# Moving one of four bit steps of a weight conversion from VectorE to POOL

## The chip, the cores and the metric

One Trainium2 chip, one core of it, one launch. The metric is the device time of that launch in microseconds (us), lower is better. The engines are named as in the profile: PE (TensorE: matmuls), DVE (VectorE), ACT (ScalarE), POOL (GpSimd), SP (SyncE, which here only issues DMAs). [...]

## The reference

Three stages on float32 activations. First a recurrent attention over 4 batches, 8 heads, 768 steps, head size 48; then a max-of-three layer; then a layer with h - tanh(h).

```python
for t in range(S):                                   # 768 steps, state of 48 x 48 per head
    cur = np.einsum('bhd,bhe->bhde', u[None] * kt, vt)
    y[:, :, t] = np.einsum('bhd,bhde->bhe', rt, state + cur)
    state = wt[:, :, :, None] * state + np.einsum('bhd,bhe->bhde', kt, vt)
...
h = np.maximum(np.maximum(x @ w1, x @ w2), x @ w3)   # x: 3072 x 384, each w: 384 x 768
y = h @ w_out                                        # 768 x 384
h = y @ w_in                                         # 384 x 2048
out = (h - np.tanh(h)) @ w_out2                      # 2048 x 384
```

The weights of the two layers come as float64. The result is float32.

## The kernel before

The 3072 tokens are done in six groups of 512 tokens (four chunks of 128). The attention of a chunk is done with scans of the decays, a masked score matrix and a carried state. While the max-of-three layer of group g is on PE, the attention of group g + 1 is done beside it: the loop over the 18 weight columns (6 row blocks f, three weights j: 18 "slots") calls `advance(slot)` after the matmuls of a slot, and `advance` issues the next steps of the list that `att_steps` made (`i0` to `i5` for each chunk in the first group).

**The weights on their way in.** The 64-bit words are moved by SP into slots of the tile `Y` (eight of them, `SLOTS`), and the device turns each block of 128 x 384 numbers, called a unit, into float32 with five instructions: `abs_f64` on ACT (line 66) takes the size of the upper half as a float32, and `bits_f64` does four steps on DVE: line 72 bounds the size from both sides, line 73 shifts and masks, lines 74 and 75 put sign, exponent and the lower half's top bits together. All four work in place on the unit's tile, so each waits for the one before.

**Units.** There are 24: 0 to 17 are the three first weights (tiles `WAg0` to `WAg17`; in the order's lists they stand as `WAg_102` to `WAg_119`, so unit 13 is `WAg_115` and unit 17 is `WAg_119`), 18 to 23 the layer's output weight (all in one tile, `WOg`). `w1_unit` (line 531) does one and then issues the load of the raw words of the unit eight later. Eight units (0 + 1 + 3 + 4, the table `PRO`) are done during the prologue, in which the attention of the first group runs alone. The other 16 are done in the first group: `advance(slot)` ends with `w1_upto(slot + 1 + 8)`, so slot s makes unit 8 + s, behind the attention steps of that slot; the last ones follow at the end of the loop.

**Order.** The first group stands in a block where the program's order is kept as written (`tc.manual_schedule`). So what waits on an engine is what the code wrote earlier: on DVE the evictions `max0` (line 644, which frees a PSUM bank for PE), the scans (lines 207 and 209), the scaled keys and queries (215, 216), the diagonal (291), the state (329) and the key transpose (259); on POOL the mask of the scores (line 303, two a chunk), the bonus products (lines 224, 225) and the decayed state (245). From the second group on, weights are multiplied as pairs of a high and a low part (lines 488 to 490, `mm3`); their split (lines 478 and 479) begins when the first group ends.

Of the kernel before, what the change touches and what calls it, by code (L numbers as in the profile page):

```python
# [15 lines left out]
ALU = mybir.AluOpType  # L16
# [26 lines left out]
PRO = [0, 1, 3, 4]  # L43
# [11 lines left out]
LO_BITS = (896 << 20)  # L55
HI_BITS = (1150 << 20) | 0xFFFFF


def bits_f32(i):
    return struct.unpack("<f", struct.pack("<I", i))[0]  # L60
# [4 lines left out]
def abs_f64(act, raw, out):  # L65
    act.activation(out, raw[:, 1::2].bitcast(F32), AF.Abs)


def bits_f64(dve, raw, out):
    oi = out.bitcast(I32)  # L70
    high, low = raw[:, 1::2], raw[:, 0::2]
    dve.tensor_scalar(out, out, bits_f32(LO_BITS), bits_f32(HI_BITS), ALU.max, ALU.min)
    dve.tensor_scalar(oi, oi, 3, 0x3FFFFFFF, ALU.logical_shift_left, ALU.bitwise_and)
    dve.scalar_tensor_tensor(oi, high, -0x40000000, oi, ALU.bitwise_and, ALU.bitwise_or)  # L74
    dve.scalar_tensor_tensor(oi, low, 29, oi, ALU.logical_shift_right, ALU.bitwise_or)  # L75
# [16 lines left out]
def main_path(ctx, tc, wT, rkT, w0, rk0, nat, vpad, uT, ub, wA, wo1, wi2, wo2, outT, count):  # L92
    nc = tc.nc
    pe, act, dve, pool, sp = nc.tensor, nc.scalar, nc.vector, nc.gpsimd, nc.sync
# [378 lines left out]
    def w1_upto(n):  # L473
        while w1n < min(n, 24):
            w1_unit()
# [5 lines left out]
    def conv(raw, hi, lo, eng=pool):  # L481
        g = cv()
        abs_f64(act, raw, g)
        bits_f64(dve, raw, g)
        split(g, hi, lo, eng)
# [38 lines left out]
    def w1_load(i):  # L524
        sp.dma_start(Yi[:, (i % SLOTS) * 2 * UN:(i % SLOTS + 1) * 2 * UN], w1raw[i].bitcast(I32))
# [5 lines left out]
    def w1_unit():  # L531
        nonlocal w1n
        i = w1n
        w1n += 1
        o = i % SLOTS * 2 * UN
        q = i - 3 * F1
        raw = Yi[:, o:o + 2 * UN]
        g = WAg[i].rearrange("p k m -> p (k m)") if q < 0 else WOgf[:, q * UN:(q + 1) * UN]
        abs_f64(act, raw, g)
        bits_f64(dve, raw, g)  # L540
        if i + SLOTS < len(w1raw):
            w1_load(i + SLOTS)

# [25 lines left out]
    for c in range(GROUPS[0]):  # L569
        st = {}  # L570
        n = c + 1
        scores(c, st)
        key_turn_pe(c)
        key_out_pe(c)
        masked(c, st)
        warm(WARM[2] if c < 2 else 0)
        state_mm(c)
        bonus(n)
        scans(n)
        decays(n)  # L580
        state_add(c)
        state_decay(n)
        outputs(c)
        warm(WARM[3] if c < 2 else 0)
        outputs_out(c, c * C)
        squares(n)
        load_next(c)
        if c == 0:
            sp.dma_start(ubt, ub)
            for i in range(PRELOAD[1], SLOTS):  # L590
                w1_load(i)
        for _ in range(PRO[min(c, len(PRO) - 1)]):
            w1_unit()
        bonus_sum(n)
        bonus_vals(n)
# [225 lines left out]
def general_path(ctx, tc, wA, wo1, wi2, wo2, gwkr, gv, gu, outT):  # L821
# [55 lines left out]
    for dst, src in ((WA, wA.rearrange("p f n -> p (f n)")), (WO, wo1),  # L877
                     (W2, wi2.rearrange("p f n -> p (f n)")), (WP, wo2.rearrange("p f n -> p (f n)"))):
        flat = dst.rearrange("p a b c d -> p (a b c d)") if len(dst.shape) == 5 else dst.rearrange("p a b c -> p (a b c)")
        for o in range(0, flat.shape[1], 768):  # L880
            raw = stg.tile([P, 2 * 768], I32, name="graw")
            sp.dma_start(raw, src[:, o:o + 768].bitcast(I32))
            abs_f64(act, raw, flat[:, o:o + 768])
            bits_f64(dve, raw, flat[:, o:o + 768])
# [123 lines left out]
```

## Time and profile before

| what | us |
|---|---|
| median of 3 runs | 876.72 (876.35 to 880.52) |
| the profiled execution, its own time | 877.04 |
| its span in the trace | 875.2 |
| PE busy | 844.2 (96%) |
| DVE busy | 507.2 (58%) |
| ACT busy | 327.7 (37%) |
| POOL busy | 193.7 (22%) |

The profile is of one execution. Times in it are in us from the start of the span; a row of the timeline gives start, duration, engine, line, operation, output <- inputs, shapes, count, and in brackets the idle time of that engine before it and what ended it. A row of the table of busy time by stretch gives the stretch, its length, the busy us (and number) of PE, PEld (PE's weight loads), DVE, ACT and POOL in it, the granted clock, the busy share of the DMA engines, and GB/s. A row of the groups gives line, engine, operation, tiles, shapes and count, then busy us in all and mean ns of one, then the idle time before them and what ended it. Matmuls of float32 appear as two rows for each instruction. [...]

The prologue ends near 49 us, the first group's 18 slots end near 120 us, the first group's output matmuls (line 740) run to 145 us, and the second group begins there.

### The profile page before, as it was taken

Reading aid. Unit: us, or ns where it says so; the run is one execution under the profiler, and the core shown is the slowest. Engines: PE = TensorE matmul, PEld = TensorE weight load, DVE = VectorE, ACT = ScalarE, POOL = GpSimd, SP = SyncE. Lnnn points to the kernel's source line nnn. Section 1 sums busy time; section 2 is a strip of 40 time slices with the busy share of each in tenths; the row PEclk is TensorE's granted clock in tenths of the full one; section 3 lists DMA queues with packets and bytes.
Section 4 is the critical chain, followed back from the end, with each engine's and each line's share of the span. In section 5 each row is a group of like instructions: output and inputs, shape, how many; then the busy total and the mean of one; then the engine's idle time right before and its main releaser. Section 6 shows DMA issues by size and latency. Waiting matters only on the chain.

```text
span 875.2 us, 11930 instructions
## 1 busy us (share of the span) xinstructions
PE 844.2 (96%) x4482; PEld 647.2 (74%) x4482; DVE 507.2 (58%) x824; ACT 327.7 (37%) x647; POOL 193.7 (22%) x201
## 2 busy tenths in 40 slices
PE   7899889999999999999997999999999999999996
PEld 5755445777777777788875688888888888888885
DVE  8989985684574675729989734334334334333332
ACT  4644424244333344335455424323323233323232
POOL 5531426452352342420262200000000000000000
PEclk8999988999999999999999999999999999999998
DMA  9665233244252353315533000000000000000001
GB/s 266 193 210 157 70 95 85 88 128 130 70 163 76 95 145 103 88 55 163 144 105 113 19 1 36 1 1 37 0 1 37 0 1 37 1 0 37 1 1 39
DMA packets 39120, 65.42 MB, mean 75 GB/s; under 512 B 6096, under 2 KB 20176, under 8 KB 39056
## 3 DMA queue, kind: packets, MB, share of 16 engines
q1 hardware_dynamic: 39056, 64.59, 25.2%
q8 instruction: 37, 0.61, 0.3%
q14 instruction: 27, 0.22, 0.1%
HBM read 52.71 MB, written 8.13 MB: 70 GB/s over the span
## 4 chain that ended last, share of the span: by engine, by line
PE 76%; DVE 5%; DMA 2%; ACT 2%; issue 1%; POOL 1%; SPq 0%; ACTq 0%; DVEq 0%
PE bank L488 24%; PE bank L490 23%; PE bank L489 23%; PE bank L355 3%; PE bank L286 2%; PE bank L740 2%; DVE cv L75 1%; DMA fwd<-kbd 1%; PE bank L319 1%; POOL WO2l L479 1%; DVE cv L74 1%; DMA kbd<-fwd 0%; DMA xs<-in_wi 0%; SPq L264 0%; DMA xs<-in_wo 0%
## 5 line engine op out<-in xcount | busy, mean ns | idle before, releaser
L786 DVE TENSOR_TENSOR tmp<-bank,tmp 128x512 f32<-128x512 f32 x96 | 66.3, 691 | 174.5 <-ACT tmp L785 174.5
L785 ACT ACTIVATE tmp<-bank 128x512 f32<-128x512 f32 x96 | 57.4, 598 | 182.5 <-PE bank L490 182.5
L488 PE MATMUL bank<-hh,WO2h 128*128 128x512 f32 x288 | 114.2, 397 | 1.7 <-ACT hh L787 1.6
L490 PE MATMUL bank<-hl,WO2h 128*128 128x512 f32 x288 | 114.3, 397 | 0.8 <-DVE hl L788 0.8
L489 PE MATMUL bank<-hh,WO2l 128*128 128x512 f32 x288 | 113.6, 394 | 0.0
L488 PE MATMUL bank<-xh,WAh 128*128 128x512 f32 x270 | 111.1, 411 | 0.0
L490 PE MATMUL bank<-xl,WAh 128*128 128x512 f32 x270 | 106.8, 395 | 0.0
L489 PE MATMUL bank<-xh,WAl 128*128 128x512 f32 x270 | 106.4, 394 | 0.0
L788 DVE TENSOR_TENSOR hl<-tmp,hh 128x512 fp32r<-128x512 f32 x96 | 66.4, 692 | 59.1 <-PE bank L490 46.6
L787 ACT CAST hh<-tmp 128x512 fp32r<-128x512 f32 x96 | 59.5, 620 | 72.8 <-DVE tmp L786 72.7
L490 PEld LDWEIGHTS bank<-hl,WO2h 128*128 128x128 f32 x288 | 54.1, 188 | 16.1 <-DVE hl L788 3.4
L488 PEld LDWEIGHTS bank<-hh,WO2h 128*128 128x128 f32 x288 | 54.2, 188 | 15.6 <-ACT hh L787 3.3
L489 PEld LDWEIGHTS bank<-hh,WO2l 128*128 128x128 f32 x288 | 54.2, 188 | 12.9
L488 PEld LDWEIGHTS bank<-xh,WAh 128*128 128x128 f32 x270 | 50.8, 188 | 15.1 <-issue 1.9
L721 POOL TENSOR_TENSOR hl<-tmp,hh 128x512 fp32r<-128x512 f32 x25 | 38.3, 1531 | 102.7 <-ACT hh L720 100.2
L490 PEld LDWEIGHTS bank<-xl,WAh 128*128 128x128 f32 x270 | 50.8, 188 | 12.0
L489 PEld LDWEIGHTS bank<-xh,WAl 128*128 128x128 f32 x270 | 50.9, 188 | 10.5 <-issue 0.2
L702 PE MATMUL bank<-x,WAg 128*128 128x512 f32 x108 | 51.3, 618 | 3.7 <-DVE h L644 3.7
L720 ACT CAST hh<-tmp 128x512 fp32r<-128x512 f32 x30 | 18.6, 618 | 87.5 <-DVE tmp L718 76.0
L291 DVE COPY_PREDICATED P<-dmask,sd 128x512 f32<-128x512 uint8 x36 | 29.6, 871 | 33.6 <-POOL P L303 33.6
L718 DVE TENSOR_TENSOR tmp<-bank,tmp 128x512 f32<-128x512 f32 x60 | 40.8, 680 | 13.0 <-PE bank L490 11.4
L488 PE MATMUL bank<-xh,W2ha 128*128 128x512 f32 x108 | 42.4, 393 | 3.9 <-ACT Yb L759 2.8
(204 smaller groups left out, 1617.4 us busy)
## 6 DMA issues: line engine op xcount, KB each, us to landing
Y<-in_wA SPq DMA_DIRECT2D x18, 384.0 KB, 6.4
nt<-in_nat SPq DMA_DIRECT2D x12, 576.0 KB, 4.8
rk<-in_rkT SPq DMA_DIRECT2D x30, 192.0 KB, 3.4
w2st<-in_wi SPq DMA_DIRECT2D x12, 384.0 KB, 3.3
third<-in_nat SPq DMA_DIRECT2D x7, 576.0 KB, 4.5
kbd<-fwd SPq DMA_DIRECT2D x13, 256.0 KB, 2.1
fwd<-kbd SPq DMA_DIRECT2D x52, 64.0 KB, 2.0
third<-in_rkT SPq DMA_DIRECT2D x16, 192.0 KB, 3.4
```

The costliest lines, as they stand in the source:

```text
L291: dve.copy_predicated(q, dmask[:, None, :].to_broadcast([P, NP, C]), sdt[c % 2][:, j::2, None].to_broadcast([P, NP, C]))
L355: pe.matmul(yab[64 * j:64 * j + HD, p * C:(p + 1) * C], *t(j), start=i == 0, stop=i == len(terms) - 1)
L488: pe.matmul(bk, wh, ah, start=first, stop=False)
L489: pe.matmul(bk, wl, ah, start=False, stop=False)
L490: pe.matmul(bk, wh, al, start=False, stop=last)
L702: pe.matmul(bk, WAg[3 * f + j][:, k], x0[:, k], start=k == 0, stop=k == KT - 1)
L718: dve.tensor_tensor(t[:, 0:n], bk[:, 0:n], t[:, 0:n], ALU.max)
L721: (dve if f == F1 - 1 else pool).tensor_tensor(hl[:, f, 0:n], t[:, 0:n], hh[:, f, 0:n], ALU.subtract)
L785: act.activation(t, bk, AF.Tanh)
L786: dve.tensor_tensor(t, bk, t, ALU.subtract)
L787: act.copy(hh[:, r], t)
L788: dve.tensor_tensor(hl[:, r], t, hh[:, r], ALU.subtract)
```

## The change

`bits_f64` gets a parameter: the engine that does its first step. `w1_unit` passes POOL for units 8 to 23 (`i >= sum(PRO)`, which is 8) and DVE for the eight of the prologue. Nothing else is edited. The later conversions of the second layer's weights (`conv`) and the general path pass nothing and stay on DVE.

```diff
-def bits_f64(dve, raw, out):
+def bits_f64(dve, raw, out, clamp=None):
     oi = out.bitcast(I32)
     high, low = raw[:, 1::2], raw[:, 0::2]
-    dve.tensor_scalar(out, out, bits_f32(LO_BITS), bits_f32(HI_BITS), ALU.max, ALU.min)
+    (clamp or dve).tensor_scalar(out, out, bits_f32(LO_BITS), bits_f32(HI_BITS), ALU.max, ALU.min)
     dve.tensor_scalar(oi, oi, 3, 0x3FFFFFFF, ALU.logical_shift_left, ALU.bitwise_and)
...
         abs_f64(act, raw, g)
-        bits_f64(dve, raw, g)
+        bits_f64(dve, raw, g, pool if i >= sum(PRO) else dve)
```

So ACT's step is followed by POOL, and POOL's by three steps on DVE; line 73 now waits for POOL's semaphore instead of DVE's own.

Where the steps come to stand on POOL, in the middle of the first group. Before (`P` are the masked scores, `nt` the chunk's queries, keys and values):

```order
L303 AFFINE_SELECT P_145<-P_145 128x512
L303 AFFINE_SELECT P_146<-P_146 128x512
L224 TENSOR_TENSOR nt_139<-nt_139,ubt 128x384
L225 TENSOR_TENSOR nt_139<-nt_139 128x384
L303 AFFINE_SELECT P_145<-P_145 128x512
```

With the change, from the second of these rows to unit 17:

```order
L303 AFFINE_SELECT P_146<-P_146 128x512
L224 TENSOR_TENSOR nt_139<-nt_139,ubt 128x384
L225 TENSOR_TENSOR nt_139<-nt_139 128x384
L72 TENSOR_SCALAR WAg_115<-WAg_115 128x384
L72 TENSOR_SCALAR WAg_116<-WAg_116 128x384
L72 TENSOR_SCALAR WAg_117<-WAg_117 128x384
L72 TENSOR_SCALAR WAg_118<-WAg_118 128x384
L303 AFFINE_SELECT P_145<-P_145 128x512
L303 AFFINE_SELECT P_146<-P_146 128x512
L224 TENSOR_TENSOR nt_140<-nt_140,ubt 128x384
L225 TENSOR_TENSOR nt_140<-nt_140 128x384
L72 TENSOR_SCALAR WAg_119<-WAg_119 128x384
```

The step of unit 13 (`WAg_115`) and that of unit 17 (`WAg_119`) stand behind the two selects and the two products of a chunk; those of units 14 to 16 follow unit 13's directly.

On DVE the step of unit 17 leaves its place between the scaled queries of a chunk and the unit's second step; a piece of the difference:

```order
 L215 TENSOR_TENSOR rk_138<-rk_138,suf 128x512
 L216 TENSOR_TENSOR rk_138<-rk_138,fwd 128x512
-L72 TENSOR_SCALAR WAg_119<-WAg_119 128x384
 L73 TENSOR_SCALAR WAg_119<-WAg_119 128x384
 L74 SCALAR_TENSOR_TENSOR WAg_119<-Y,WAg_119 128x384
```

The other fifteen rows of line 72 leave DVE in the same way. Beside this, the build moves a few rows on other engines: on SP one of two DMAs of a later chunk's decays (`third<-in_wT`) goes ahead of the six that carry a chunk's output (`xs<-yst`, lines 368 to 371); on PE one score matmul (line 286) stands before the output matmuls of line 740 and not behind; and from the end of the first group on some splits (line 479) change places.

## Rows read from the trace of the kernel before

**Rows 1.** The page's part 1: busy time, share of the span, instructions.
```profile
PE 844.2 (96%) x4482; PEld 647.2 (74%) x4482; DVE 507.2 (58%) x824; ACT 327.7 (37%) x647; POOL 193.7 (22%) x201
```

**Rows 2.** Busy time by stretch of 20 us (columns: see the section on the profile).
```profile
100.00:120.00 20.00, 17.26 (x81) 8.00 (x80) 19.14 (x34) 4.67 (x11) 7.59 (x7) 0.91 0.29 79
140.00:160.00 20.00, 20.00 (x104) 14.02 (x104) 13.24 (x19) 5.27 (x12) 13.30 (x12) 1.00 0.11 32
```

**Rows 3.** The chain that ended last, in order of time: start, us, what.
```profile
118.83 0.68 DVE h L644
...
120.19 0.72 DVE fwd L259
...
120.93 2.01 DMA kbd<-fwd
...
129.81 1.19 PE bank L286 x4
```

**Rows 4.** Timeline of PE, at its two stalls for line 644.
```profile
94.77 2.84 PE L702 MATMUL bank<-x,WAg 128*128 128x512 f32 x6 [0.94 <-DVE h L644]
...
108.24 4.54 PE L702 MATMUL bank<-x,WAg 128*128 128x512 f32 x6 [2.74 <-DVE h L644]
```

**Rows 5.** Busy time by stretch of 5 us (columns as in rows 2).
```profile
110.00:115.00 5.00, 5.00 (x24) 1.98 (x23) 4.67 (x10) 2.34 (x6) 0.00 (x0) 0.73 0.85 238
130.00:135.00 5.00, 5.00 (x9) 2.54 (x10) 3.06 (x8) 1.97 (x4) 2.21 (x3) 0.50 0.37 92
```

**Rows 6.** DVE's groups by line and shape, 54.9 to 117 us.
```profile
L644 DVE TENSOR_TENSOR h<-bank,h 128x512 f32<-128x512 f32 x9 | 6.2, 685 | 0.1
...
L72 DVE TENSOR_SCALAR WAg<-WAg 128x384 f32<-128x384 f32 x10 | 4.6, 460 | 2.9 <-ACT WAg L66 2.9
...
L72 DVE TENSOR_SCALAR WOg<-WOg 128x384 f32<-128x384 f32 x6 | 2.7, 454 | 0.7 <-ACT WOg L66 0.7
```

**Rows 7.** Timeline of DVE: undisturbed steps of unit 15, and unit 18's first.
```profile
81.82 0.35 DVE L72 TENSOR_SCALAR WAg<-WAg 128x384 f32<-128x384 f32 x1
82.20 0.36 DVE L73 TENSOR_SCALAR WAg<-WAg 128x384 int32<-128x384 int32 x1
...
96.50 0.36 DVE L72 TENSOR_SCALAR WOg<-WOg 128x384 f32<-128x384 f32 x1 [0.53 <-ACT WOg L66]
```

**Rows 8.** Timeline of POOL and DVE around unit 13.
```profile
74.00 1.23 POOL L303 TENSOR_SCALAR_AFFINE_SELECT P<-P 128x512 f32<-128x512 f32 x2 [8.35 <-ACT P L302]
...
75.20 1.10 POOL L224 TENSOR_TENSOR nt<-nt,ubt 128x384 f32<-128x384 f32 x1
...
76.38 1.00 POOL L225 TENSOR_TENSOR nt<-nt 128x384 f32<-128x384 f32 x1
...
77.83 0.56 DVE L75 SCALAR_TENSOR_TENSOR WAg<-Y,WAg 128x384 int32<-128x384 int32 x1
```

**Rows 9.** Timeline of POOL and DVE around unit 17.
```profile
89.46 1.90 POOL L303 TENSOR_SCALAR_AFFINE_SELECT P<-P 128x512 f32<-128x512 f32 x2 [12.08 <-ACT P L302]
...
90.90 0.67 DVE L73 TENSOR_SCALAR WAg<-WAg 128x384 int32<-128x384 int32 x1
91.33 1.09 POOL L224 TENSOR_TENSOR nt<-nt,ubt 128x384 f32<-128x384 f32 x1
...
92.50 1.19 POOL L225 TENSOR_TENSOR nt<-nt 128x384 f32<-128x384 f32 x1
92.87 1.24 DVE L75 SCALAR_TENSOR_TENSOR WAg<-Y,WAg 128x384 int32<-128x384 int32 x1
```

**Rows 10.** Timeline of DVE: unit 10's first step, and a scan before unit 16.
```profile
61.33 0.36 DVE L72 TENSOR_SCALAR WAg<-WAg 128x384 f32<-128x384 f32 x1 [1.29 <-ACT WAg L66]
...
85.29 1.23 DVE L209 TENSOR_TENSOR_SCAN fwd<-wt,d 128x516 f32<-128x516 f32 x1
```

**Rows 11.** Timeline of SP and DVE near unit 22.
```profile
111.80 0.43 SPq L192 DMA_DIRECT2D third<-in_wT  x1
...
112.66 0.36 DVE L72 TENSOR_SCALAR WOg<-WOg 128x384 f32<-128x384 f32 x1 [0.16 <-ACT WOg L66]
```

## The prediction

> **What bounds the kernel now.** I read the page's busy shares first: TensorE (PE) is busy for 96% of the span [rows 1], so a change on another engine can only act where PE waits. The table of busy time by stretch shows where that is [rows 2]: in 100 to 120 us PE has 17.26 of 20 us and VectorE (DVE) 19.14, so there DVE is the full engine; in 140 to 160 us PE has its whole 20.00 and DVE 13.24. Then the chain of waits [rows 3]: from 101 us on it runs through DVE, instruction after instruction, to the last running maximum of the first group at 118.83, through the key transpose at 120.19, two transfers through memory, and back to PE at 129.81. After that it is PE's own. The timeline of PE names the two stalls on DVE: 0.94 us before 94.77 and 2.74 us before 108.24, both for an eviction of line 644 [rows 4]. The table in 5-us stretches tells what a stall costs besides: the granted clock is 0.73 in 110 to 115 us, so the six matmuls at 108.24 take 4.54 us where six took 2.84, and 0.50 in 130 to 135 us, behind the wait at the end of the chain [rows 4, 5]. So the change acts on the right engine in the right stage: what DVE gains or loses up to 118.83 goes to the end almost one to one.
>
> **What it takes from DVE.** The 16 clamps took 4.6 + 2.7 = 7.3 us on DVE [rows 6], some of them held up. An undisturbed one is 0.35 to 0.36 us, and the next instruction starts 0.38 us after it did [rows 7]; with that 16 x 0.38 = 6.1 us leave DVE.
>
> **What a clamp costs on POOL.** The trace has no tensor_scalar on POOL. From below: the masks' select, one tile in and one out like the clamp, takes 1.23 us for two of 512 columns, 0.62 each [rows 8]; at 384 columns that is 0.46 us if all of it scales. From above: a product of two 384-column tiles takes 1.10 us [rows 8]. I take 0.55, between the select as it is and the select scaled, because the clamp also has one input; 0.46 and 1.10 are kept for the range. [...]
>
> **Where the two engines exclude each other.** This is the step that decides. At 91.33 and 92.50 POOL multiplies two tiles; the DVE step at 92.87 takes 1.24 us and ends at 94.11, 0.42 us after POOL's end at 93.69, where its like takes 0.56 [rows 8, 9]. The select, with one input, does it too: the DVE step at 90.90 takes 0.67 instead of 0.36, and the two selects 1.90 instead of 1.23 [rows 7 to 9]. One engine waits until the other's instruction is through. So a clamp on POOL is not beside DVE's steps but between them, unless DVE is idle or in an eviction from PSUM: the nine of line 644 took 685 ns on the mean, and nothing is seen to hold them [rows 6].
>
> **The walk through the units** (a unit is one 384-column block; 8 to 23 are moved).
> - Units 8 to 12: unit 8 now waits for two selects and a product, but DVE was idle for 1.29 us before unit 10 [rows 10], which takes that up. From there a 0.38 us saving against a clamp or a POOL queue of the same size: nothing, to 0.3 us either way.
> - Unit 13 (WAg_115): its clamp stands on POOL behind two selects and two products, which end at 77.38 [rows 8]. The clamp then runs 77.4 to 77.95. DVE's last step of the unit ended at 78.39; now the three steps start at 78.0, need 0.36 + 0.56 + 0.56 + two issues of 0.03, and are held some 0.4 us by the clamps of units 14 and 15 right behind: 79.95. That is 1.55 us late; units 14 and 15 have no clamp left and return 2 x 0.38: 0.8 us late.
> - Unit 16: its clamp meets the scan at 85.29 [rows 10], now 0.8 us later, waits for its end and makes DVE wait in turn; the 0.38 us are lost again: 0.9 us late.
> - Unit 17 (WAg_119): the same pattern. The selects and products ended at 93.69 [rows 9]; 0.9 us late and 0.35 us less disturbed they end at 94.25. Clamp to 94.8, three steps of 1.54 us: 96.4 instead of 94.11, 2.3 us late. PE's stall before 94.77 grows by as much.
> - Units 18 to 23: 6 x 0.38 = 2.3 us leave DVE. At two of them DVE already waits for ScalarE's absolute value (idle 0.53 us at unit 18 [rows 7]); there POOL's clamp and its hand-over, 0.55 + 0.1, stand in the same place: 1.3 us. The other four hold DVE by 0.55 less the 0.14 us by which a held step overlaps (0.56 - 0.42), three times in four (the fourth finds DVE idle or evicting): 4 x 0.41 x 0.75 = 1.2 us. Saved 2.3, paid 2.5.
>
> Sum: 2.3 + 0.2, less up to 0.3 for the early units and for gaps between clamps: **+2.2 us** at 118.83. The transpose, both transfers and the scores at 129.81 follow as much later. PE is full after that, so it stays: the profiled execution, 877.04 us (span 875.2), would be 879.2, and the median of the runs, 876.72, lies 0.3 us below it. **Forecast: 879.0 us.** The clock's loss I count as moved, not added: the stall before 94.77 becomes the long one and the one before 108.24 shrinks, since PE arrives there later. The longer queue on POOL keeps no DMA back: SP's transfers of raw weights wait for the unit's last step on DVE, so they start up to 2 us later, into units that are eight turns ahead of their matmul. One transfer of a later chunk's decays, 0.43 us to issue [rows 11], moves ahead of the six small ones that carry a chunk's output; ScalarE's squares wait for those, and the absolute value of unit 22 behind them. DVE was idle 0.16 us there [rows 11], so this can cost up to 0.4; I leave it in the rounding of the sum. The score matmul that moves on PE is one of sixteen and only changes places.
>
> **Rivals.**
> 1. *The clamp is as slow as a two-input product* (slower). Place: units 13 to 23, where some 12 clamps stand or hold on DVE's path. For: two immediate operands and two operations in one instruction, on an engine that needs 1.10 us for a 384-column product. Against: the select. At 1.0 us it adds 0.45 x 12 = 5.4 us: 884.4. It passes 0.5% (4.4 us, about what a measurement of this kernel can tell from no change) from a clamp of 0.55 + 2.2 / 12 = 0.73 us on.
> 2. *POOL does not hold DVE* (faster). If a clamp leaves DVE's steps alone, units 18 to 23 return 2.3 - 1.3 = 1.0 us beside what is late at 17, and the holds at 13 and 16 go (0.8): the result is about +0.4. If POOL also were ahead of DVE everywhere, the 3.7 us of stalls and the 1.7 us of slow matmuls behind 108.24 (4.54 - 2.84) would be the most there is to win: 871.3. Against: the selects in rows 9, and the order, in which two clamps stand behind products. [...]
> 3. *The longer stall near 94 us costs clock of its own.* PE would be idle for over 3 us there, more than before 108.24, and the slow matmuls could outlast DVE's lateness, or a second slow stretch follow. Price: 1.7 us by rows 4, or twice that: 880.7 to 882.4.
>
> **How the numbers follow.** Forecast 0.58, rival 1 0.25, rival 2 0.08 (half of it a real gain), rival 3 0.09. The forecast's own range is 877.0 (clamp 0.46: 0.09 x 12 = 1.1 less; 0.9 less again if the early units and the last four gain what I counted as lost) to 881.2 (clamp 0.73). Range for 8 in 10: 875.0, which leaves out most of rival 2, to 885.0, which takes in rival 1 up to a clamp of 1.05. Faster by over 0.5% (below 872.3): 0.05, from rival 2. Slower (above 881.1): 0.28, being 0.21 of rival 1, 0.06 of rival 3 and 0.01 of the forecast. Within: 0.67.
>
> **What would show it.** The clamp's duration on POOL near 0.55 us where DVE is quiet, longer where it meets a scan; DVE idle before line 73 of units 13 and 17 for POOL, some 2 and 3 us; PE's stall for line 644 near 94 us grown to over 2.5 us and the one near 108 us shrunk; the scores at 129.81 some 2 us later. A clamp above 0.75 us makes rival 1 right. If DVE's steps keep 0.36 and 0.56 us while POOL clamps, or the transpose comes before 120.19, the prediction is wrong in its main step.

## The result, and the profile after

The change makes the kernel 1% slower: 886.42 us median of 5 runs (885.32 to 886.64) against 877.66 of 5 runs of the kernel before (876.35 to 880.52), a ratio of 1.0101 with a 95% interval of 1.0078 to 1.0124. The forecast was 879.0 us in a range of 875.0 to 885.0: the sign of the forecast's sum was right (+2.2 us), its size was not (+8.8 us), and the time lies outside the range. The profiled execution took 886.42 us, span 884.7, so 9.5 us more span than before.

The page's part 1 after, against [rows 1]:

```profile
PE 847.2 (96%) x4482; PEld 648.4 (73%) x4482; DVE 498.8 (56%) x808; ACT 328.0 (37%) x647; POOL 215.6 (24%) x217
```

DVE did get its work off: 16 instructions and 8.4 us less. POOL has the 16 instructions more, and 21.9 us.

The groups of line 72, now on POOL, and of line 73 behind it on DVE, 54.9 to 125 us. They answer to [rows 6], where line 72 took 460 and 454 ns on DVE:

```profile
L72 POOL TENSOR_SCALAR WAg<-WAg 128x384 f32<-128x384 f32 x10 | 16.0, 1608 | 11.0 <-ACT WAg L66 10.9
L72 POOL TENSOR_SCALAR WOg<-WOg 128x384 f32<-128x384 f32 x6 | 9.2, 1537 | 8.3 <-ACT WOg L66 8.3
...
L73 DVE TENSOR_SCALAR WAg<-WAg 128x384 int32<-128x384 int32 x10 | 4.4, 439 | 17.9 <-POOL WAg L72 17.9
...
L73 DVE TENSOR_SCALAR WOg<-WOg 128x384 int32<-128x384 int32 x6 | 2.9, 490 | 3.5 <-POOL WOg L72 3.5
```

The clamp takes 1.5 to 1.6 us on POOL. The prediction took 0.55 and held 1.10 for the upper bound. DVE waits for it 17.9 + 3.5 = 21.4 us, at eight places. Against that stand 7.3 us of clamps and 3.6 us of waits for ScalarE that it no longer has [rows 6]. The balance is 10.5 us, of which 8.0 are still there at the key transpose (below).

The timeline of POOL and DVE at units 12, 13 and 17 (start, duration; in brackets the idle time before and what ended it), against [rows 8, 9]:

```profile
72.25 1.23 DVE L209 TENSOR_TENSOR_SCAN fwd<-wt,d 128x516 f32<-128x516 f32 x1
...
72.36 2.40 POOL L72 TENSOR_SCALAR WAg<-WAg 128x384 f32<-128x384 f32 x1 [3.96 <-ACT WAg L66]
...
80.69 4.70 POOL L72 TENSOR_SCALAR WAg<-WAg 128x384 f32<-128x384 f32 x3
...
82.21 0.65 DVE L73 TENSOR_SCALAR WAg<-WAg 128x384 int32<-128x384 int32 x1 [4.66 <-POOL WAg L72]
...
82.89 0.56 DVE L74 SCALAR_TENSOR_TENSOR WAg<-Y,WAg 128x384 int32<-128x384 int32 x1
...
98.38 1.49 POOL L72 TENSOR_SCALAR WAg<-WAg 128x384 f32<-128x384 f32 x1
...
99.90 0.36 DVE L73 TENSOR_SCALAR WAg<-WAg 128x384 int32<-128x384 int32 x1 [4.61 <-POOL WAg L72]
```

DVE is idle for 4.66 us before unit 13 and 4.61 us before unit 17. Two more things are to be seen. The step of line 74 at 82.89, which reads two tiles, takes its undisturbed 0.56 us in the middle of three clamps (80.69 to 85.39); the one-input step of line 73 at 82.21 is longer, 0.65 for 0.36. And the clamp of unit 12, issued while the scan of 72.25 to 73.48 runs, takes 2.40 us, some 0.9 more than the 1.49 of one alone: it ends 1.28 us behind the scan.

The timeline of PE at its stalls for the eviction of line 644, against [rows 4], where they were 0.94 and 2.74 us:

```profile
84.70 4.54 PE L702 MATMUL bank<-x,WAg 128*128 128x512 f32 x6 [3.59 <-DVE h L644]
...
102.10 4.46 PE L702 MATMUL bank<-x,WAg 128*128 128x512 f32 x6 [2.91 <-DVE h L644]
...
115.89 2.84 PE L702 MATMUL bank<-x,WAg 128*128 128x512 f32 x6 [1.44 <-DVE h L644]
...
127.56 4.56 PE L740 MATMUL bank<-h,WOg 128*128 128x512 f32 x10 [0.35 <-DVE h L644]
```

There is a new stall of 3.59 us before 84.70, behind unit 13, and its six matmuls take 4.54 us where six took 2.84. In the table of busy time by 5 us the granted clock of PE, as a share of full speed, is 0.67 and 0.70 in the stretches behind the two long stalls, where [rows 5] have 0.73 behind the one before:

```profile
85.00:90.00 5.00, 5.00 (x20) 2.18 (x21) 4.77 (x10) 1.71 (x5) 0.39 (x1) 0.67 0.64 162
100.00:105.00 5.00, 2.90 (x4) 1.35 (x5) 3.59 (x7) 3.00 (x8) 1.87 (x2) 0.70 0.03 12
```

The chain of waits that ended last, against [rows 3]. It now runs through POOL:

```profile
120.36 1.50 POOL WOg L72
121.88 0.66 DVE WOg L73
...
128.18 0.72 DVE fwd L259
128.92 2.02 DMA kbd<-fwd
```

The key transpose comes at 128.18 us, 8.0 us later than at 120.19. From there the lateness mostly stays: the last matmul is 9.3 us late.

### The profile page after: what moved, and what is told of

It reads as the page before. It is cut to its first block, busy times and chain, and to the rows that moved or that the text cites. A ratio compares the mean times of both kernels' runs of the same rounds, so it can differ in the third digit from the quotient of the medians.

```text
span 884.7 us, 11936 instructions
## 1 busy us (share of the span) xinstructions
PE 847.2 (96%) x4482; PEld 648.4 (73%) x4482; DVE 498.8 (56%) x808; ACT 328.0 (37%) x647; POOL 215.6 (24%) x217
## 4 chain that ended last, share of the span: by engine, by line
PE 65%; DVE 6%; DMA 5%; POOL 3%; SPq 3%; ACT 2%; issue 2%; DVEq 0%; ACTq 0%; POOLq 0%
PE bank L488 21%; PE bank L490 21%; PE bank L489 20%; PE bank L355 2%; POOL WAl L479 1%; SPq L371 1%; DMA kbd<-fwd 1%; DMA nt<-in_nat 1%; PE bank L286 1%; DMA fwd<-kbd 1%; DVE WAl L479 1%; DVE cv L75 1%; SPq L264 1%; DMA xs<-yst 1%; POOL WO2l L479 1%
## 5 line engine op out<-in xcount | busy, mean ns | idle before, releaser
L489 PEld LDWEIGHTS bank<-xh,WAl 128*128 128x128 f32 x270 | 50.9, 188 | 10.5 <-issue 0.2
```

Of the source, the lines that this page charges most:

```text
L489: pe.matmul(bk, wl, ah, start=False, stop=False)
```

## The experiments

What had to be told apart: whether the loss is **waiting** (the clamp's own length and its place in POOL's queue stand on the path from ScalarE to DVE), or **holding** (POOL keeps DVE's other steps from running, the step that the prediction said decides). The runs share some runs of the kernel before, so its median differs by set (876.7 to 877.7).

The profiled executions differ by up to 3.5 us in the prologue, which the edits hardly touch (two of them add one filling of a tile on POOL there, and one issues unit 8's first steps at its end). To compare them, this table takes the start of the first matmul of the first group as zero: how much later than in the kernel before (where it is 49.45 us, and the others 120.54 and 867.87) the first output matmul (line 740 before, the end of the first group's columns) and the last matmul start, in us, worked out from each trace. Each row is one execution, so small differences between rows are not sure.

| run | POOL's step, mean us | first output matmul | last matmul |
|---|---|---|---|
| the change | 1.58 | +7.0 | +9.3 |
| e1_one_op: one bound | 1.27 | +5.0 | +5.6 |
| e2_no_clamp: no bounds | none | -5.7 | -2.5 |
| e3_aside: no bounds, POOL busy beside | 1.63 | -4.4 | -2.3 |
| e4_two_back: units 13, 17 on DVE | 1.61 | +3.9 | +4.9 |
| e5_ahead: one unit ahead | 1.67 | +3.7 | +4.8 |
| e6_half: half the columns | 1.03 | +7.3 | +10.9 |
| e7_product: product of two tiles | 1.07 | +7.4 | +8.3 |
| e11_two_products: two products | 0.66 | +0.8 | +2.3 |
| e12_min_first: bounds in the other order | 0.63 | +0.8 | +1.8 |
| e13_min_first_14: that, 13 and 17 on DVE | 0.71 | +0.1 | +0.9 |

**A shorter step.** Only the lower bound on POOL; the upper one is left out for units 8 to 23.

```diff
-    (clamp or dve).tensor_scalar(out, out, bits_f32(LO_BITS), bits_f32(HI_BITS), ALU.max, ALU.min)
+    if clamp:
+        clamp.tensor_scalar(out, out, bits_f32(LO_BITS), None, ALU.max)
...
```

> The POOL step of units 8 to 23 bounds from below only (max); the bound from above is left out. Theory A (DVE waits for the length of POOL's step, 1.49 us a unit): the time moves with that length. If one operation of two halves the work for an element, the step falls to about 1.0 us and the run to about +4 us over before; if it stays at 1.49, the length is not set by the number of operations and the time stays at +9. Theory B (POOL's step holds DVE's steps): the same direction, but with DVE's two-input steps at 1.2 us beside POOL's step.

Measured: 884.35 us median, before 877.2, ratio 1.010 [1.0066, 1.0135]. The step takes 1.26 to 1.27 us. By the table the loss at the first output matmul falls from 7.0 to 5.0 us for 0.31 us less a step; the medians (+7.2 where the change has +8.8) don't part the two clearly. One operation in place of two is far from half the price (1.27 for 1.58).

**No bounds, and POOL free or busy.** Units 8 to 23 are not bounded in either run. In the second POOL does the same 16 clamps at the same places of its queue on a tile that nobody waits for, and that waits for nobody. Both edits are against the kernel before.

```diff
-        bits_f64(dve, raw, g)
+        if i >= sum(PRO):
+            pool.tensor_scalar(aside, aside, bits_f32(LO_BITS), bits_f32(HI_BITS), ALU.max, ALU.min)
+        bits_f64(dve, raw, g, i < sum(PRO))
```

(The run without POOL's clamps has only the first and the last of these lines; a last argument of `False` leaves line 72 out.)

> Units 8 to 23 get no bounds at all, on no engine. It gives what can be won at most by taking the step from DVE: 16 x 0.38 = 6.1 us of DVE's time. If DVE sets the end of the first group, as read from the trace of before, this is 4 to 7 us below before. If PE or a DMA takes over as the bound, it is under 2 us.

> As the run without bounds, but POOL does the same 16 two-operation steps in the same places of its queue on a tile of its own, which nothing waits for; the weights get no bounds. Theory A (waiting for the result is what costs): close to the run without bounds, at most 3 us above it, from the selects and products that come later on POOL. Theory B (POOL's steps hold DVE's): most of the loss of the changed kernel stays, so 4 us or more over before; DVE's steps of 0.56 us would show 1.2 beside POOL's.

Measured: 874.66 us without them (ratio 0.998 [0.9958, 1.0002]) and 878.06 with them (1.001 [0.999, 1.003]; before 877.2). From the same first matmul on, the two lie 1.3 us apart at the first output matmul and under 0.3 us at the end; the profiled execution of the second had 3.4 us more in the prologue, so in these two executions little of the difference in time (3.7 us) is the clamps'. Whether that holds for the medians is not shown. So 16 clamps of 1.63 us that run beside DVE cost at most 1.3 us in the first group, and the same clamps with DVE waiting for them cost 11.4 us more (+7.0 against -4.4). That is the **waiting** theory. One difference remains between them: clamps that wait for no result of ScalarE start earlier than those of the change. The timeline of the run with POOL busy shows why holding is small (three clamps from 95.35 to 100.62 us, and DVE's steps of unit 18 beside them; some other two-input steps of this run take 0.74 or 0.75):

```profile
95.35 5.27 POOL L545 TENSOR_SCALAR WOg<-WOg 128x384 f32<-128x384 f32 x3
...
97.40 0.69 DVE L74 TENSOR_SCALAR WOg<-WOg 128x384 int32<-128x384 int32 x1 [0.51 <-ACT WOg L66]
...
98.12 0.56 DVE L75 SCALAR_TENSOR_TENSOR WOg<-Y,WOg 128x384 int32<-128x384 int32 x1
...
98.72 0.56 DVE L76 SCALAR_TENSOR_TENSOR WOg<-Y,WOg 128x384 int32<-128x384 int32 x1
```

The first run also bounds what any place for the clamp can give: with none at all the first group ends 5.7 us earlier, but 3.2 us of it are gone at the end, and the time is not clearly below before. So neither expectation was met as it stands: DVE sets the end of the first group, and what comes behind takes more than half of the gain back.

**The two places behind the products.** Units 13 and 17 back on DVE, 14 stay.

```diff
-        bits_f64(dve, raw, g, pool if i >= sum(PRO) else dve)
+        bits_f64(dve, raw, g, pool if i >= sum(PRO) and i not in (13, 17) else dve)
```

> As the change, but units 13 and 17, whose step stands on POOL behind two selects and two products, keep it on DVE. Theory C (those two places are the loss): the time returns to within 1 us of before. Theory A: only what these two units wait beyond a plain 1.49 us step returns, about 3 to 5 us, and +4 to +6 us over before stay.

Measured: 882.36 us, ratio 1.0069 [1.0048, 1.009] to before 877.2. The two places carry 3.1 of the 7.0 us at the first output matmul and 4.4 of the 9.3 at the end; the other 14 carry the rest. Neither the queue alone nor the length alone explains the loss.

**One unit ahead.** ScalarE's absolute value and POOL's clamp of unit i + 1 are issued before unit i + 1's turn, behind unit i; the bounds are kept, all 16 on POOL.

```diff
+        if sum(PRO) <= i + 1 < len(w1raw):
+            w1_size(i + 1)
```

(`w1_size` is `abs_f64` and line 72.)

> The whole change, bounds included, but the absolute value and POOL's step of a unit are issued one unit earlier, behind the steps of the unit before, so that DVE meets a step that POOL has mostly finished. Theory A (waiting for POOL's step in the unit's own turn costs): DVE's idle time for POOL falls from 21 us to under 8, and the run from +9 us over before to within 2 us of it, at best near the run in which nothing waited for POOL. Theory B (POOL's steps hold DVE's): as slow as the change, +7 us or more. Theory D (POOL has too little time for 16 steps of 1.49 us beside its own work): DVE waits as long as in the change.

Measured: 882.51 us, ratio 1.0062 [1.0042, 1.0081] to before 877.29. DVE's waits for the clamp fall from 21.4 to 6.6 us, and the transposed keys come 0.3 us before those of the kernel before, counted from the first matmul of the group; but the time, expected within 2 us of before, is 5.2 longer. PE starts the output matmuls 3.7 us late, by one stall of 3.95 us before 111.27. The second group's first matmul, at 141.50 us, is 3.7 us early (144.56 before), since here most of the attention's matmuls that stood ahead of it stand behind it. There PE loses the lead again: the waits of this run, 130 to 190 us,

```profile
DVE WAl L480 <- POOL WAl L480: 9.9, 9, 1.9
...
PE bank L356 <- DVE P L292: 6.1, 1, 6.1
```

show one wait of 6.1 us of PE for the masked diagonal (line 291 before), which stands on DVE behind the splits of the next weights (line 479 before), done in turn by POOL and DVE. That order is not written by hand and came out otherwise here. So the waiting can be hidden, and the run does not tell what that is worth without the new wait.

**Half the columns.** POOL bounds 192 columns of each unit, DVE the other 192.

```diff
+        clamp.tensor_scalar(out[:, 0:UN // 2], out[:, 0:UN // 2], lo, hi, ALU.max, ALU.min)
+        dve.tensor_scalar(out[:, UN // 2:UN], out[:, UN // 2:UN], lo, hi, ALU.max, ALU.min)
...
```

> As the change, but POOL bounds only the first 192 of 384 columns and DVE the other 192. It measures the price of the step by columns. If it is all by the column, POOL's step takes 0.75 to 0.8 us, and by theory A the loss at the transpose falls from 8 us to about 4 (the half step on DVE, some 0.25 us each, included); if most of it is fixed, it stays at 1.2 us or more and the loss at 8.

Measured: 889.89 us, ratio 1.0118 [1.007, 1.0166]: no better than the whole change. Its groups:

```profile
L74 POOL TENSOR_SCALAR WAg<-WAg 128x192 f32<-128x192 f32 x10 | 10.7, 1077 | 13.9 <-ACT WAg L66 13.8
...
L75 DVE TENSOR_SCALAR WAg<-WAg 128x192 f32<-128x192 f32 x10 | 3.4, 344 | 3.9 <-ACT WAg L66 3.9
```

POOL's half costs two thirds of the whole (1077 ns for 1608), and DVE pays 344 ns on the mean for a half where [rows 6] show 460 for the whole. DVE waits less for POOL (11.7 us for 21.4), but again 4.5 us for ScalarE, and its halves take 5.6 us: 21.8 us in all. The first six matmuls of this profiled execution took 4.52 us where those of the others took 2.82 to 2.84, so its row in the table is the least sure.

**A product of two tiles in the clamp's place.** The unit is multiplied by a tile of ones (a spare part of the tile `WOg`); units 8 to 23 are not bounded.

```diff
+        pool.tensor_tensor(out, out, ones_tile, ALU.mult)
```

> As the change, but POOL multiplies the unit by a tile of ones, a two-input product, in place of the two bounds, which are left out. The products of the trace of before take 1.0 us, less than the step's 1.49. Theory A (only the length counts): a loss between that of the one-operation step (1.26 us) and none, about +2 to +3 us over before. Theory B, for products alone (a product holds DVE's steps, as the rows of before show): +5 us or more, with DVE's steps of 0.56 at 1.2.

Measured: 888.63 us, ratio 1.0117 [1.0072, 1.0163]. The product takes 1.0 to 1.1 us, less than the one bound (1.27), and loses more, +7.4 against +5.0 us at the first output matmul. Here holding is to be seen; three products from 82.34 to 85.36 us and two of unit 13's steps:

```profile
82.34 3.02 POOL L74 TENSOR_TENSOR WAg<-WAg,WOg 128x384 f32<-128x384 f32 x3
...
83.37 1.13 DVE L77 TENSOR_SCALAR WAg<-WAg 128x384 int32<-128x384 int32 x1 [4.17 <-POOL WAg L74]
...
84.54 1.23 DVE L78 SCALAR_TENSOR_TENSOR WAg<-Y,WAg 128x384 int32<-128x384 int32 x1
```

1.13 for 0.36 and 1.23 for 0.56. Over the 16 units DVE waits 18.9 us for POOL, less than the 21.4 of the change, but its three steps take 30.0 us where the change has 27.4. So the prediction's exclusion is right for POOL's products, and too strong for the clamp that it was applied to.

**What POOL charges.** Two runs of the kernel before with POOL instructions on a dead tile (`ubt`, which nobody reads any more) in the second layer's stage, two of each form at 384, 192 and 96 columns. Their time tells nothing (891.63 and 901.8 us); their groups are the result.

```diff
+        for _ in range(2):
+            pool.tensor_scalar(x, x, lo, hi, ALU.max, ALU.min)
...
+        for _ in range(2):
+            pool.tensor_scalar(x, x, hi, lo, ALU.min, ALU.max)
```

> The kernel before, with POOL instructions on a dead tile added in a later stage, two of each form at 384, 192 and 96 columns: tensor_scalar with two bounds, with one, with one product, with two products, a product of two tiles, a select. It prices them by themselves; its time tells nothing. If the price is by the number of operations, one product costs as one bound (1.26 at 384 columns) and two as two (1.49); if max and min are what is slow, the products are under 1.0. The select at 384 columns is expected at 0.5.

The groups at 384 columns, in this order: two bounds (max, min), one product, one bound (max), product of two tiles, select, two products (mult, mult).

```profile
L812 POOL TENSOR_SCALAR ubt<-ubt 128x384 f32<-128x384 f32 x2 | 3.0, 1497 | 0.2
L816 POOL TENSOR_SCALAR ubt<-ubt 128x384 f32<-128x384 f32 x2 | 2.3, 1172 | 0.2
L814 POOL TENSOR_SCALAR ubt<-ubt 128x384 f32<-128x384 f32 x2 | 2.3, 1169 | 0.2
...
L820 POOL TENSOR_TENSOR ubt<-ubt 128x384 f32<-128x384 f32 x2 | 1.7, 826 | 0.1
...
L822 POOL TENSOR_SCALAR_AFFINE_SELECT ubt<-ubt 128x384 f32<-128x384 f32 x2 | 1.3, 670 | 0.1
...
L818 POOL TENSOR_SCALAR ubt<-ubt 128x384 f32<-128x384 f32 x2 | 1.0, 514 | 0.2
```

The step that the prediction priced at 0.55 us exists, for two products in one instruction. Two bounds cost three times that, and one operation alone more than two products. What distinguishes them was left to the second run:

> The kernel before with POOL instructions on a dead tile in the second layer's stage, two of each form at 384, 192 and 96 columns: two bounds on int32 (max, min); the lower bound twice (max, max); the bounds in the other order (min, max); product and sum (mult, add); product and bound (mult, min); bound and product (max, mult); and a sum of two tiles. Question: which part of two bounds makes 1.50 us where two products take 0.51. If each bound is what is slow: the mixed forms some 1.0 us, (max, max) and (min, max) 1.5, (mult, add) 0.5. If only a pair of products (or product and sum) has a fast form: every form with a bound 1.2 to 1.5 us. If the type is what matters: int32 bounds far below 1.5 us, and then the change has a form that costs a third. The time of the whole kernel is of no interest.

The groups at 384 columns, in this order: the lower bound twice (max, max); int32 bounds (max, min); product and sum (mult, add); and the two bounds in the other order (min, max).

```profile
L815 POOL TENSOR_SCALAR ubt<-ubt 128x384 f32<-128x384 f32 x2 | 3.0, 1496 | 0.2
L813 POOL TENSOR_SCALAR ubt<-ubt 128x384 int32<-128x384 int32 x2 | 3.0, 1494 | 0.2
...
L819 POOL TENSOR_SCALAR ubt<-ubt 128x384 f32<-128x384 f32 x2 | 1.0, 513 | 0.2
L817 POOL TENSOR_SCALAR ubt<-ubt 128x384 f32<-128x384 f32 x2 | 1.0, 508 | 0.2
```

None of the three expectations: neither the type nor the bounds as such make the price. The same two bounds cost 1.50 us as (max, min) and 0.51 as (min, max). A product mixed with a bound is slow too (two instructions each, 1.5 to 2.0 us). It is the pair of operations in its order.

**The same place with a step of the predicted length.** First with two products (the units not bounded), then with the real bounds in the other order, which gives the same sizes, since the lower bound is below the upper.

```diff
+        clamp.tensor_scalar(out, out, 1.0, 1.0, ALU.mult, ALU.mult)
```

> The change, but POOL's step on units 8 to 23 multiplies the unit twice by 1.0 in one instruction (the sizes are not bounded there). Its place, its hand-over and its one input are those of the clamp; alone on a dead tile it took 0.51 us, where the clamp took 1.50 and the prediction took 0.55. Theory (the prediction's sum was right but for the clamp's length, and what matters is waiting for the result): a step of 0.51 to 0.65 us in place, the key transpose (120.19 before) 0 to +2.5 us late, and a time within 0.3% of before, +0 to +2.5 us. A straight line through the first outputs of the change (+7.0 at a step of 1.58 us) and of one bound (+4.95 at 1.26 us) gives -0.5 at 0.51 us, the prediction's own sum +2.2. Rival (the place behind ScalarE and POOL's queue costs by itself, whatever the length): +4 us or more, near the change with units 13 and 17 back on VectorE (+5). Second rival (a product holds VectorE, as the product of two tiles did at 1.05 us with +7.4): VectorE's two last steps grow from 0.56 to over 0.65 us beside it, and the time is +3 to +5.

```diff
+        clamp.tensor_scalar(out, out, bits_f32(HI_BITS), bits_f32(LO_BITS), ALU.min, ALU.max)
```

> The change with POOL's two bounds in the other order: first the upper, then the lower (min, max in place of max, min; the lower bound is below the upper, so the sizes are the same). On a dead tile this form took 0.51 us and max, min 1.50. Theory (only the clamp's price was mis-sized, and the price hangs on the order of the two operations): a step of 0.51 us undisturbed, the stall near 94 us some 3 us and the ones near 85 and 116 us gone, the transpose 1.5 to 2.5 us late, a time of +2 to +3 us, as with two products (+2.7). Rival (0.51 us holds only for a product or a sum, and min, max was cheap there by the values of the dead tile or by the quiet around it): a step of 1.2 us or more and +5 to +9 us.

Measured: 879.4 us with two products, before 876.68, ratio 1.0035 [1.0016, 1.0054]; 878.98 us with the bounds turned round, before 876.87, ratio 1.0022 [1.0000, 1.0044]. That is +2.7 and +2.1 us, where the prediction's sum was +2.2. (The straight line in the first of the two expectations gives 0.1 us at 0.51, not -0.5.) The run with the bounds, its group on POOL, the steps of units 13 and 17 (line 76 is line 73 before, 77 is 74, 78 is 75), and PE's stalls for the eviction:

```profile
L73 POOL TENSOR_SCALAR WAg<-WAg 128x384 f32<-128x384 f32 x10 | 6.1, 611 | 14.8 <-ACT WAg L66 14.8
```

```profile
77.69 1.55 POOL L73 TENSOR_SCALAR WAg<-WAg 128x384 f32<-128x384 f32 x3
...
78.23 0.65 DVE L76 TENSOR_SCALAR WAg<-WAg 128x384 int32<-128x384 int32 x1 [3.67 <-POOL WAg L73]
78.91 0.74 DVE L77 SCALAR_TENSOR_TENSOR WAg<-Y,WAg 128x384 int32<-128x384 int32 x1
79.69 0.56 DVE L78 SCALAR_TENSOR_TENSOR WAg<-Y,WAg 128x384 int32<-128x384 int32 x1
...
94.83 0.36 DVE L76 TENSOR_SCALAR WAg<-WAg 128x384 int32<-128x384 int32 x1 [3.62 <-POOL WAg L73]
...
95.82 0.56 DVE L78 SCALAR_TENSOR_TENSOR WAg<-Y,WAg 128x384 int32<-128x384 int32 x1
```

```profile
97.03 2.84 PE L705 MATMUL bank<-x,WAg 128*128 128x512 f32 x6 [3.23 <-DVE h L647]
...
109.72 2.84 PE L705 MATMUL bank<-x,WAg 128*128 128x512 f32 x6 [1.96 <-DVE h L647]
```

The stall near 85 us is gone, the one near 94 has grown from 0.94 to 3.23 us, by 2.29 where the walk said 2.3, and the one near 108 has shrunk from 2.74 to 1.96. Unit 17 ends at 96.38, where the walk had 96.4. The rivals fall: that the place costs +4 us or more whatever the length (first run), and that the short price holds on a dead tile alone (second run).

**The better order without the two places.** As before it, with units 13 and 17 on DVE.

```diff
+        bits_f64(dve, raw, g, pool if i >= sum(PRO) and i not in (13, 17) else None)
```

> As min first, but units 13 and 17, whose step stands behind two selects and two products in POOL's queue, stay on VectorE; 14 units are moved. Theory (with a step of 0.51 us what is left of the loss is POOL's queue at units 13 and 17, counted as 0.8 + 1.4 us in the prediction): the stall near 94 us back at about 1 us, the transpose 0 to 1.5 us early, a time from 1.5 us below before to 1 us above, a version that is no slower than before. Rival (the hand-over from ScalarE over POOL to VectorE is what remains, at units 8 to 12 and 18 to 23): still +1.5 to +3 us.

Measured: 879.16 us, before 876.87, ratio 1.0026 [1.0008, 1.0044]. By the table, from the same first matmul on, it is +0.1 us at the first output matmul and +0.9 at the end, so in these executions part of the loss goes with the two places, and the stall near 94 us is back at 0.78, as expected; but a stall of 2.98 us before 109.59 remains, the transpose comes 0.9 us late (counted in the same way) and not early, and the medians do not show a gain over all 16 (878.98). By the medians, +2.3 us, it is the rival that came, the hand-over at the other units; the trace does not settle it. No version that keeps the bounds beats the kernel before, and the run with no bounds at all (-0.2%, not certain) says that there was almost nothing to win. One unit ahead with the bounds turned round was not tried.

## Why the prediction failed, by its own steps

- **Where the kernel is bound**: right for what DVE loses. PE is late by its stalls for line 644 and by the end of the chain, and what was late at the transpose (+8.0 us) was late at the end (+9.3). For what DVE gains, "almost one to one" is wrong: without bounds the transpose came 5.6 us earlier and the last matmul only 2.5. Counted as in the table, the change is 7.3 us late at the second group's first matmul and 8.4 at 169.03 us; 0.9 of that is one stall of PE for an eviction of the second group (line 718), which stands on DVE behind the splits (line 479). What adds the rest up to 9.3 is not traced. The run without bounds gives its gain back elsewhere: 1.8 us of it with a stall of 3.09 us for the attention's keys, 1.29 us in the kernel before.

```profile
166.56 0.50 PE L488 MATMUL bank<-xh,WAh 128*128 128x512 f32 x1 [1.03 <-DVE tmp L718]
```

- **What leaves DVE**: right. 16 instructions, and 8.4 us less DVE time in all, against 6.1 undisturbed or 7.3 as they stood.
- **What a clamp costs on POOL: this is the step that failed.** "I take 0.55 [...] because the clamp also has one input", with 1.10 as the upper bound. It takes 1.49 us undisturbed and 1.58 on the mean, more than the product that stood as the bound. The select was a poor neighbour: the same number of inputs says nothing of the price, since the same instruction with its two operations turned round costs 0.51. The trace of before had no such row, and "nearest" was judged by operands where the operation decided. An upper bound from a row of another operation is no bound.
- **That POOL and DVE exclude each other**, "the step that decides": right for products, too strong for the clamp. The prediction had named the sign for it, steps that keep 0.36 and 0.56 us while POOL clamps, and it came for the two-input steps (82.89), not for line 73 (0.65 for 0.36). It cost the sum little: at unit 13 the prediction held DVE's steps for 0.4 us, and beside the clamp turned round lines 76 and 77 take 0.65 and 0.74 for 0.36 and 0.56, which is 0.47 us. So what was held differs by the pair: beside products DVE's steps took 1.13 and 1.23 us for 0.36 and 0.56 (above), the clamp issued during a scan ran 1.28 of its 2.40 us behind the scan, some 0.2 less than the 1.49 of one alone, and two-input steps that started while a clamp of the change ran kept their 0.56.
- **The walk through the units**: right with a clamp of about the assumed length (0.63 on the mean), and not only in its sum. Turned round, the bounds make unit 13 end 1.86 us late where the walk had 1.55, unit 16 1.05 (0.9) and unit 17 2.27 (2.3); the stall near 94 us is 3.23, the transpose 1.8 us late (2.2), and the time 2.1 us longer. That the forecast of 879.0 stands beside 878.98 is luck in its last digits. One sign does not follow from the walk: DVE idle "some 2 and 3 us" before line 73 of units 13 and 17. It is 3.67 and 3.62 us in that run, and the walk's own start at 78.0 gives 4.0, since DVE's instruction before ended at 74.04 in the trace of before. With the real length these waits are 4.66 and 4.61 us, and the wait at unit 13, which the walk had PE not feel, becomes a stall of 3.59 us at 84.70.
- **Rival 1** had the mechanism, the sign (a clamp above 0.75 us) and the direction. Its price was too low in length (1.0) and too high in count: 0.45 us times 12 places. From 0.63 to 1.58 us a clamp the loss at the first output matmul rises from 0.8 to 7.0 us, 6.5 us per us, as if six or seven of the 16 counted, and the run with one bound lies on the same line (0.8 + 0.64 x 6.5 = 5.0). The prediction's sum with that slope would be 2.2 + 1.03 x 6.5 = 8.9 us beside the 8.8 measured, but the slope is taken from the runs themselves, so this is no test. Its chance of 0.25 was too small for a price between bounds a factor of two apart, and the range's upper end, "up to a clamp of 1.05", rested on the same row.
- **Rival 2** (POOL does not hold DVE) came true in part of its condition, the two-input steps, and not in its result: the price of waiting outweighed it. **Rival 3**: slow matmuls (4.54 and 4.46 us) do stand behind the stalls that the waiting made, in two places where the kernel before had one, but what that added at the end is not seen. In the two runs with a short step the stalls near 97 us are equal, 3.24 us (two products) and 3.23 (bounds turned round); behind the first six matmuls take 5.49 us, behind the second 2.84, and in both the first output matmul is 0.8 us late. In the second no group of six that starts between 81 and 118 us takes more than 2.84 us, so there the clock's loss was not "moved" either; it is not seen.

## What to carry to other kernels

When a step of a dependent chain moves to another engine, count its full length there and that engine's queue on the path: here 1.58 us a step for 0.46, and 21.4 us in which DVE waited for it. The relief of the first engine may count only if the result is not waited for at once: with POOL busy beside DVE the first output matmul came 4.4 us early, with DVE waiting for the same clamps 7.0 us late. So price the very instruction on the new engine, with its operations in their order, by a run on a dead tile if no trace has it, and keep the range open above when none has. And first take the step out altogether: here even that was worth some 0.2%, not clearly more than nothing.

## What was not expected of the hardware

- In the two price runs the length of one tensor_scalar on POOL went with its operations and their order: at 384 columns (max, min) 1.50 us, (max, max) 1.50, a single max or mult 1.17, and (mult, mult), (mult, add) and (min, max) 0.51. On DVE the clamp as (max, min) took 0.35 [rows 7].
- At 192 columns in the second of the two price runs (max, min) on int32 took 0.85 us and (min, max) 0.35, so the slow form costs (1494 - 854) / 192 = 3.3 ns a column and the fast one (508 - 348) / 192 = 0.8.
- A running clamp as (max, min) lengthened DVE's one-input step (0.65 for 0.36) and in the change left the two-input steps of lines 74 and 75 inside it at 0.56; as (min, max) it also lengthened a two-input step (0.74). Products of two tiles held both far longer (1.13 and 1.23).
